# Linear attention and a feed-forward product on one core: all chunks in pairs, 64-row products side by side, earlier DMA transposes, an order that counts the queue's rows

## Chip, cores, metric

One core of a Trainium2 chip. The metric is the device time of one execution in microseconds (us), the median of several runs. The kernel before takes 196.92 us (196.65 to 197.27, 4 runs; the prediction was made against 196.75, the median of the first 3).

## The reference, cut to what matters

```python
# r, k, v, w: (4, 8, 768, 48) f32; u: (8, 48); w_in: (384, 2048); w_out: (2048, 384)
for t in range(S):                                   # per batch and head, state is 48 x 48
    cur = einsum('bhd,bhe->bhde', u * k_t, v_t)
    y[:, :, t] = einsum('bhd,bhde->bhe', r_t, state + cur)
    state = w_t[..., None] * state + einsum('bhd,bhe->bhde', k_t, v_t)
x = y.transpose(0, 2, 1, 3).reshape(3072, 384)
h = x @ w_in
out = maximum(0.01 * h, h) @ w_out
```

## The kernel before

The sequence is cut into 24 chunks of 128 steps (6 per batch entry). A chunk is done by matrix products: cumulative sums of log w, decayed r and k, their transposes, masked scores, an inner product with v, an outer product that feeds the state. The feed-forward part runs chunk by chunk beside it. Before any instruction is emitted, a small list scheduler (`Plan.order`) puts all steps of all engines in one order, from priorities and guessed durations; each engine then runs its part in that fixed order.

Chunks 0 to 5 are done as three *pairs*, 6 to 23 as *singles*. A pair loads two time steps per partition (runs of 384 B in place of 192 B), and so its time axis is interleaved: it works on two 64-row halves (`ab`) and two interleaved chunks (`j`, `jt`, `js`).

```python
NPE = 14; LEAD = 4; PAIRS = (0, 2, 4)        # DMA transposes from chunk index 14
WEIGHTS = [(2, 4.0)] * 2 + [(4, 24.0)] * 4 + [(6, 44.0)] * 2
yp_r = pp_r = ring("yp", 1, [128, 512], F32, psum)      # one bank for outer and inner
...                                          # pair(n):
for ab in range(2):                          # outer: one half, then (later) the other
    pp = yp_r.take()
    for p in range(NP):
        for j in range(2):
            nc.tensor.matmul(pp.t[:, p*2*D:(p+1)*2*D],            # 64 x 128 tile
                lhsT=rk[j].t[q0:q0+64, 1, 2*p:2*p+2, :], rhs=vb[j].t[q0:q0+64, 2*p:2*p+2, :], ...)
...
for p in range(NP):                          # scores of one jt: 32 matmuls, 64 x 64 tiles
    for js in range(2):
        for q in (0, 64):
            for par in range(2):
                nc.tensor.matmul(sc[par].t[q:q+64, p, 64*js:64*js+64], ...)
...
for ab in range(2):                          # state: 8 matmuls, 128 x 64 tiles
    for p in range(NP):
        nc.tensor.matmul(yp.t[q:q+64, 2*p*D:(2*p+2)*D], lhsT=rkT[jt].t[:, p, q:q+64], rhs=sbs[ab]..., ...)
for h in range(H):                           # inner: 32 matmuls, 64 x 64 tiles
    for js in range(2):
        for ab in range(2):
            nc.tensor.matmul(yp.t[q:q+64, h*D:(h+1)*D], lhsT=m.t[q:q+64, ...], rhs=vb[js].t[q:q+64, h, :], ...)
...                                          # single(n): 8 scores, 4 outer, 4 state, 8 inner, 128 rows each
```

## Time and profile before

| | before |
|---|---|
| time, median | 196.92 us |
| span in the profile | 195.8 us |
| TensorE busy | 180.3 us (92%) |
| first matmul, first feed-forward matmul, start of the last matmul | 4.85, 23.64, 192.03 us |
| gaps on TensorE between them | 7.2 us, all before 46.1 us |

The prediction shows the lines. How to read them: TensorE (PE) is busy nearly all the time, but its records overlap, since matmuls are pipelined (twelve L808 are shown with 0.83 us, and the next group starts 0.67 after them). What it has to issue is better read from starts: the *issue time* of a group below is the time from each matmul's start to the next one's, gaps taken off. Added up over this trace it is 180.0 us.

### The profile page before, as it was taken

The page shows a single profiled execution, that of the slowest core. Times are in us where ns is not written, and L with a number is a line of the kernel's source. Part 1 is how long each engine was busy: PE and PEld are TensorE (multiplying, and loading weights), DVE is VectorE, ACT ScalarE, POOL GpSimd, SP SyncE. Part 2 cuts the span into 40 slices and gives each one's busy share as a digit, 9 for nine tenths or more (in the row PEclk, how much of TensorE's full clock was granted, in tenths as well). Part 3 has the DMA queues.
Part 4 walks back from the last instruction along what each step waited for, and adds up shares of the span by engine and source line. Part 5 has one row for each costly group of instructions (what it writes and reads, how often), then busy time and mean ns, then how long its engine had stood idle before and what let it go on. Part 6 is the DMA issues. An engine that isn't in the chain of part 4 may idle for free.

```text
span 195.8 us, 6457 instructions
## 1 busy us (share of the span) xinstructions
PE 180.3 (92%) x2680; PEld 141.3 (72%) x2680; DVE 129.6 (66%) x228; ACT 119.2 (61%) x256; POOL 109.0 (56%) x148
## 2 busy tenths in 40 slices
PE   0978399987999999999999999999999999999993
PEld 0355398784778878877877877877878778778771
DVE  2399955599698897976768568666869676541111
ACT  3655267577665876775878675757654656334430
POOL 7598905187997999889638647547534202100000
PEclk9999759999999999999999999999999999999999
DMA  6999998999998999786487696999942614711012
GB/s 160 300 327 293 380 313 243 244 255 190 186 258 174 217 223 209 157 172 136 112 159 162 146 197 146 204 177 179 201 94 64 142 49 116 97 60 55 11 41 82
DMA packets 109280, 33.92 MB, mean 173 GB/s; under 512 B 102593, under 2 KB 107714, under 8 KB 109250
## 3 DMA queue, kind: packets, MB, share of 16 engines
q1 hardware_dynamic: 109250, 33.50, 75.8%
q8 instruction: 21, 0.34, 0.7%
q14 instruction: 9, 0.07, 0.1%
HBM read 25.17 MB, written 4.72 MB: 153 GB/s over the span
## 4 chain that ended last, share of the span: by engine, by line
PE 83%; SPq 7%; DMA 4%; DVE 3%; issue 1%; ACT 1%; DVEq 0%
PE hp L808 33%; PE op L860 32%; SPq L460 5%; DMA in<-in_moe_w_in_dram 4%; PE se L738 3%; PE yp L772 2%; PE cp L679 2%; PE so L380 1%; PE yp L642 1%; PE yp L749 1%; DVE rk L340 1%; PE yp L767 1%; PE se L380 1%; SPq L282 1%; PE yp L448 1%
## 5 line engine op out<-in xcount | busy, mean ns | idle before, releaser
L842 ACT ACTIVATE g<-hp 128x512 bf16<-128x512 f32 x96 | 57.3, 597 | 42.5 <-PE hp L808 41.7
L808 PE MATMUL hp<-xT,w_in_b 128*128 128x128 bf16 x1152 | 81.0, 221 | 0.8 <-ACT xT L455 0.8
L860 PE MATMUL op<-w_out_b,g 128*128 128x384 bf16 x384 | 77.0, 326 | 0.9 <-DVE w_out_b L305 0.9
L808 PEld LDWEIGHTS <-w_in_b 128*128 128x128 bf16 x1152 | 70.7, 99 | 8.4 <-issue 1.1
L860 PEld LDWEIGHTS <-g 128*128 128x128 bf16 x384 | 33.1, 98 | 15.0 <-issue 1.0
L361 POOL TENSOR_TENSOR vs<-in,dg 128x384 f32<-128x384 f32 x24 | 21.2, 891 | 20.9 <-DVE y L434 12.9
L349 POOL TENSOR_TENSOR ru<-in,ub 128x384 f32<-128x384 f32 x24 | 26.2, 1100 | 7.7 <-DMA in<-in_r_dram 7.7
L353 POOL TENSOR_TENSOR ru<-ru,in 128x384 f32<-128x384 f32 x24 | 26.6, 1112 | 0.4
L410 POOL TENSOR_TENSOR sb<-s,a 128x384 bf16<-128x384 f32 x15 | 13.3, 887 | 20.9 <-DVE s L424 8.9
L340 DVE TENSOR_TENSOR rk<-in,er 128x384 bf16<-128x384 f32 x24 | 18.4, 768 | 9.2 <-DMA in<-in_r_dram 5.5
L434 DVE TENSOR_TENSOR y<-yp,vs 128x384 bf16<-128x384 f32 x24 | 13.3, 555 | 12.7 <-PE yp L772 9.2
L340 DVE TENSOR_TENSOR rk<-in,ek 128x384 bf16<-128x384 f32 x24 | 21.3, 887 | 0.1
L329 POOL CAST vb<-in 128x384 bf16<-128x384 f32 x24 | 14.5, 612 | 6.2 <-issue 4.3
L876 DVE COPY o<-op 128x384 f32<-128x384 f32 x10 | 5.6, 558 | 16.9 <-PE op L860 16.7
L401 DVE TENSOR_TENSOR m<-se,maskb 128x512 bf16<-128x512 f32 x18 | 12.4, 687 | 5.6 <-PE so L738 5.4
L357 DVE TENSOR_REDUCE dg<-ru 128x8 f32<-128x384 f32 x24 | 12.8, 543 | 3.9 <-POOL ru L353 3.8
L334 ACT ACTIVATE er<-cp 128x384 f32<-128x384 f32 x21 | 10.3, 489 | 7.1 <-DVE ci L704 5.5
L324 ACT ACTIVATE lw<-in 128x384 bf16<-128x384 f32 x24 | 12.3, 520 | 2.9 <-DMA in<-in_w_dram 2.9
L704 DVE TENSOR_TENSOR ci<-cp,lw 128x384 f32<-128x384 f32 x18 | 9.9, 551 | 4.6 <-ACT xT L455 2.3
L424 DVE TENSOR_TENSOR s<-yp,sb 128x384 f32<-128x384 f32 x16 | 8.8, 552 | 5.9 <-PE yp L595 3.5
L401 DVE TENSOR_TENSOR m<-so,maskb 128x512 bf16<-128x512 f32 x18 | 12.2, 679 | 0.0
L380 PEld LDWEIGHTS <-rk 128*128 128x128 bf16 x112 | 8.6, 108 | 3.7 <-DVE rk L340 1.9
(93 smaller groups left out, 213.4 us busy)
## 6 DMA issues: line engine op xcount, KB each, us to landing
out_dram<-o SPq DMA_DIRECT2D x24, 192.0 KB, 2.2
in<-in_w_dram SPq DMA_DIRECT2D x18, 192.0 KB, 3.6
in<-in_k_dram SPq DMA_DIRECT2D x18, 192.0 KB, 3.7
in<-in_r_dram SPq DMA_DIRECT2D x18, 192.0 KB, 3.9
in<-in_v_dram SPq DMA_DIRECT2D x18, 192.0 KB, 3.7
in<-in_moe_w_in_dram SPq DMA_DIRECT2D x4, 768.0 KB, 7.6
in<-in_moe_w_out_dram SPq DMA_DIRECT2D x4, 768.0 KB, 9.6
in<-in_w_dram SPq DMA_DIRECT2D x3, 384.0 KB, 8.2
```

Of the source, the lines that this page charges most:

```text
L329: "POOL", 0.57, lambda: nc.gpsimd.tensor_copy(out=vb.t[:], in_=vn.t),
L340: lambda: nc.vector.tensor_tensor(out=rk.t[:, a, :, 0:D], in0=xn.t, in1=e.t[:], op=ALU.mult),
L349: lambda: nc.gpsimd.tensor_tensor(out=ru.t[:], in0=rn.t, in1=ubv, op=ALU.mult),
L353: lambda: nc.gpsimd.tensor_tensor(out=ru.t[:], in0=ru.t[:], in1=kn.t, op=ALU.mult),
L357: lambda: nc.vector.tensor_reduce(out=dg.t[:], in_=ru.t[:], axis=AX.X, op=ALU.add),
L361: lambda: nc.gpsimd.tensor_tensor(out=vs.t[:], in0=vn.t, in1=dg.t[:].unsqueeze(2).to_broadcast([128, H, D]), op=ALU.mult),
L401: lambda par=par: nc.vector.tensor_tensor(out=m.t[:, par], in0=sc[par].t[:], in1=mask.unsqueeze(1).to_broadcast([128, NP, 128]), op=ALU.mult),
L410: lambda: nc.gpsimd.tensor_tensor(out=sb.t[:].rearrange("p g a d -> p (g a) d"), in0=s_in.t[:].rearrange("p g a d -> p (g a) d"), in1=a_ap ...
L434: lambda: nc.vector.tensor_tensor(out=y.t[:], in0=hd(yp.t[:, 0:DM]), in1=vs.t[:], op=ALU.add),
L808: nc.tensor.matmul(hp.t[:, a * N : (a + 1) * N], lhsT=w_in_b[:, t, (j + a) * 128 : (j + a + 1) * 128], rhs=xT[:, t, c0 : c0 + N], start=(a ...
L842: lambda hp=hp, g=g, j=j, J=J, N=N: nc.scalar.activation(out=g.t[:, j : j + J, 0:N], in_=hp.t[:, 0 : J * N].rearrange("p (a n) -> p a n", ...
L860: nc.tensor.matmul(op.t[:], lhsT=g.t[:, j, off : off + 128], rhs=w_out_b[:, j, :], start=(j == 0), stop=(j == NJ - 1))
```

## The change

All chunks become pairs; the outer and state products alternate their halves, the outer's into two banks; transposes go to the DMA queue from the ninth chunk; the first pair takes banks that are still idle; weights are queued later, the row of u by ScalarE's queue; and the scheduler models a queue that holds a limited number of rows. Smaller edits of the same diff (durations in the scheduler's model, no latency between two steps of one engine, three `g` buffers in place of four) are not shown.

```diff
-            free[e] = now + self.dur[i] * (1.8 if e == "PE" and now < 18 else 1)
+            free[e] = now + self.dur[i] * (1.8 if e == "PE" and now < 26 else 1)
...
+                flying = [x for x in flying if x[0] > free[e]]
+                while sum(x[1] for x in flying) + self.rows[i] > 3300:
+                    free[e] = max(free[e], flying.pop(0)[0])
...
-    NPE = 14
-    LEAD = 4
+    NPE = 8
+    LEAD = 8
-    PAIRS = (0, 2, 4)
+    PAIRS = range(0, NCH, 2)
-    WEIGHTS = [(2, 4.0)] * 2 + [(4, 24.0)] * 4 + [(6, 44.0)] * 2
-    CASTS = 2
+    WEIGHTS = [(2, 20.15)] * 2 + [(4, 40.15)] * 4 + [(6, 44.0)] * 2
+    CASTS = 3
...
-                s_T += turn(rk[j], rkT[j], s_d[j], n, P0)
+                s_T += turn(rk[j], rkT[j], s_d[j], n, P0, (hp_r, hp_r) if j and n == 0 else (se_r, so_r))
...
+            pps = [op_r.take(), op_r.take()] if n == 0 else [se_r.take(), so_r.take()]
+            def outer():
+                for p in range(NP):
+                    for j in range(2):
+                        for ab in range(1 if last else 2):
+                            ...matmul into pps[ab], rows 64*ab to 64*ab+63...
...
-                    for ab in range(2):
-                        for p in range(NP):          # state
+                    for p in range(NP):
+                        for ab in range(2):
```

More of the change, by code (lines that the diff above doesn't have):

```diff
@@ L22, in __init__, with add @@
     def __init__(self):
-        self.eng, self.dur, self.fn, self.deps, self.pri, self.wire = [], [], [], [], [], []
-    def add(self, eng, dur, fn, deps, pri, wire=None):
+        self.eng, self.dur, self.fn, self.deps, self.pri, self.wire, self.rows = [], [], [], [], [], [], []
+    def add(self, eng, dur, fn, deps, pri, wire=None, rows=0):
         i = len(self.eng)
@@ L33, in add @@
         self.wire.append(wire)
+        self.rows.append(rows)
         return i
@@ L48, in order @@
         dma_free = 0.0
+        flying = []
         for i in range(n):
@@ L72, in order @@
             else:
+                flying = [x for x in flying if x[0] > free[e]]
+                while sum(x[1] for x in flying) + self.rows[i] > 3300:
+                    free[e] = max(free[e], flying.pop(0)[0])
                 dma_free = max(dma_free, free[e]) + self.wire[i]
                 done[i] = dma_free + 1.6
+                flying.append((done[i], self.rows[i]))
             heapq.heappush(events, (free[e], e))
@@ L77, in order @@
                 left[j] -= 1
-                ready_at[j] = max(ready_at[j], done[i])
+                same = self.eng[j] == e and self.wire[i] is None
+                ready_at[j] = max(ready_at[j], free[e] if same else done[i])
                 if not left[j]:
@@ L141 @@
     NCI = 3
-    NPE = 14
-    LEAD = 4
+    NPE = 8
+    LEAD = 8
     AHEAD = 5
-    PAIRS = (0, 2, 4)
-    PWIRE, WIRE = 1.3, 1.15
-    WEIGHTS = [(2, 4.0)] * 2 + [(4, 24.0)] * 4 + [(6, 44.0)] * 2
-    CASTS = 2
+    PAIRS = range(0, NCH, 2)
+    PWIRE, WIRE = 1.45, 1.15
+    WEIGHTS = [(2, 20.15)] * 2 + [(4, 40.15)] * 4 + [(6, 44.0)] * 2
+    CASTS = 3
     blocks = [1] * NCH
@@ L192 @@
     y_r = ring("y", 4, [128, H, D], BF16)
-    g_r = ring("g", 4, [128, NJ, max(blocks) * L], BF16)
+    g_r = ring("g", 3, [128, NJ, max(blocks) * L], BF16)
     o_r = ring("o", 4, [128, DM], F32)
     hp_r = ring("hp", 2, [128, 512], F32, psum)
-    op_r = ring("op", 2, [128, DM], F32, psum)
+    op_r = ring("op", 2, [128, 512], F32, psum)
     cp_r = ring("cp", 1, [128, 512], F32, psum)
     yp_r = pp_r = ring("yp", 1, [128, 512], F32, psum)
-    se_r = ring("se", 1, [128, NP, 128], F32, psum)
-    so_r = ring("so", 1, [128, NP, 128], F32, psum)
+    se_r = ring("se", 1, [128, 512], F32, psum)
+    so_r = ring("so", 1, [128, 512], F32, psum)
     with tc.manual_schedule():
@@ L253, with step @@
         plan = Plan()
-        def step(eng, dur, fn, pri, reads=(), writes=(), deps=(), wire=None):
+        def step(eng, dur, fn, pri, reads=(), writes=(), deps=(), wire=None, rows=0):
             d = list(deps)
@@ L259, in step @@
                 d += x.old
-            i = plan.add(eng, dur, fn, d, pri, wire)
+            i = plan.add(eng, dur, fn, d, pri, wire, rows)
             for x in (*reads, *writes):
@@ L290, in load @@
                     )
-            ld = step("SP", 0.45, load, pri, writes=[st], wire=2.0)
+            ld = step("SP", 0.45, load, pri, writes=[st], wire=2.0, rows=(384, 512)[which])
             made = []
@@ L338, in product @@
             return step(
-                "DVE", 0.6 if n < 4 else 0.84 - 0.04 * a,
+                "DVE", 0.65 if n < 2 else 0.84 - 0.04 * a,
                 lambda: nc.vector.tensor_tensor(out=rk.t[:, a, :, 0:D], in0=xn.t, in1=e.t[:], op=ALU.mult),
@@ L363, in bonus, with gt, turn @@
                 P0 + 2, reads=[vn, dg], writes=[vs], deps=[vl, s_dg])
-        def turn(rk, rkT, s_d, n, P0):
+        def gt(t):
+            return t[:].rearrange("p (g t) -> p g t", t=128)
+        def turn(rk, rkT, s_d, n, P0, banks):
             if n >= NPE:
@@ L371, in turn @@
                         out=rkT.t[:], in_=rk.t[:].rearrange("p a h d -> p (a h d)")),
-                    P0, reads=[rk], writes=[rkT], deps=s_d, wire=1.6)]
+                    P0, reads=[rk], writes=[rkT], deps=s_d, wire=1.7, rows=512)]
             made = []
             for a, eng in ((0, "DVE"), (1, "ACT")):
-                tr = (se_r, so_r)[a].take()
-                trv = tr.t[:].bitcast(BF16).rearrange("p g t -> p (g t)").rearrange("p (g t) -> p g t", t=128)
+                tr = banks[a].take()
+                trv = gt(tr.t[:].bitcast(BF16))
                 def tpose(trv=trv, a=a):
@@ L401, in masked @@
                     lambda par=par: nc.vector.tensor_tensor(
-                        out=m.t[:, par], in0=sc[par].t[:],
+                        out=m.t[:, par], in0=gt(sc[par].t),
                         in1=mask.unsqueeze(1).to_broadcast([128, NP, 128]), op=ALU.mult),
@@ L415, in shrink, with state @@
                 P0 + 1, reads=[s_in, use], writes=[sb], deps=deps)
-        def state(sx, pp, sb, P0, deps):
+        def state(sx, pp, i, sb, P0, deps):
             def f():
-                i = pp.t[:, 0:DM].rearrange("p (g a d) -> p g a d", g=NP, a=2)
                 if sb is None:
@@ L441, in finish @@
                         out=xT[:, :, col : col + L], in_=y.t[:].rearrange("p h d -> p (h d)")),
-                    P0 + 1, reads=[y], deps=[s_ye], wire=0.65))
+                    P0 + 1, reads=[y], deps=[s_ye], wire=0.65, rows=200))
                 return
@@ L460, in load_in @@
                 "SP", 0.45, lambda: nc.sync.dma_start(out=view(use), in_=src), P0 + 0.1 * i,
-                writes=[use], wire=wire, deps=[cums[n - AHEAD]] if n >= AHEAD else [])
+                writes=[use], wire=wire, rows=1024, deps=[cums[n - AHEAD]] if n >= AHEAD else [])
         def spread_u():
             u_row = step(
-                "SP", 0.45,
-                lambda: nc.sync.dma_start(out=ur[:], in_=u.rearrange("h d -> (h d)").unsqueeze(0)),
-                0.15, wire=0.05)
+                "ACT", 0.5,
+                lambda: nc.scalar.dma_start(out=ur[:], in_=u.rearrange("h d -> (h d)").unsqueeze(0)),
+                -1, wire=0.05)
             up = op_r.take()
@@ L470, in spread_u @@
                 "PE", 0.7,
-                lambda: nc.tensor.matmul(up.t[:], lhsT=onef[:], rhs=ur[:], start=True, stop=True),
-                0, writes=[up], deps=[u_row])
+                lambda: nc.tensor.matmul(up.t[:, 0:DM], lhsT=onef[:], rhs=ur[:], start=True, stop=True),
+                -1, writes=[up], deps=[u_row])
             return step(
-                "ACT", 0.5, lambda: nc.scalar.copy(out=ub[:], in_=up.t[:]), 3, reads=[up], deps=[s_ub])
+                "ACT", 0.5, lambda: nc.scalar.copy(out=ub[:], in_=up.t[:, 0:DM]), 0.05, reads=[up], deps=[s_ub])
         def weights_at(n):
@@ L571, in pair @@
             for j in range(2):
-                s_T += turn(rk[j], rkT[j], s_d[j], n, P0)
+                s_T += turn(rk[j], rkT[j], s_d[j], n, P0, (hp_r, hp_r) if j and n == 0 else (se_r, so_r))
             vs = [vs_r.take() for _ in range(2)]
             s_vs = [bonus(vs[j], rn[j], kn[j], vn[j], (kl, rl, vl), P0) for j in range(2)]
+            pps = [op_r.take(), op_r.take()] if n == 0 else [se_r.take(), so_r.take()]
[3 more added lines that the diff above has]
+                        for ab in range(1 if last else 2):
+                            q0 = 64 * ab
+                            nc.tensor.matmul(
+                                gt(pps[ab].t)[:, p, 0 : 2 * D],
+                                lhsT=rk[j].t[q0 : q0 + 64, 1, 2 * p : 2 * p + 2, :].rearrange("p h d -> p (h d)"),
+                                rhs=vb[j].t[q0 : q0 + 64, 2 * p : 2 * p + 2, :].rearrange("p a d -> p (a d)"),
+                                start=(j == 0), stop=(j == 1), skip_group_check=True)
+            s_pp = step(
+                "PE", 0.45, outer, P0 + 1, reads=[*rk, *vb], writes=pps, deps=[s_d[0][1], s_d[1][1], *s_vb])
             sbs, s_sbs = [], []
             for ab in range(2):
-                q0 = 64 * ab
                 sb, s_sb = None, []
@@ L589, in pair @@
                     break
-                pp = yp_r.take()
-                def outer(pp=pp, q0=q0):
-                    for p in range(NP):
-                        for j in range(2):
-                            nc.tensor.matmul(
-                                pp.t[:, p * 2 * D : (p + 1) * 2 * D],
-                                lhsT=rk[j].t[q0 : q0 + 64, 1, 2 * p : 2 * p + 2, :].rearrange("p h d -> p (h d)"),
-                                rhs=vb[j].t[q0 : q0 + 64, 2 * p : 2 * p + 2, :].rearrange("p a d -> p (a d)"),
-                                start=(j == 0), stop=(j == 1), skip_group_check=True)
-                s_pp = step(
-                    "PE", 0.35, outer, P0 + 1, reads=[*rk, *vb], writes=[pp],
-                    deps=[s_d[0][1], s_d[1][1], *s_vb])
+                pp = pps[ab]
                 sx = sx_r.take()
-                prev = (sx, [state(sx, pp, sb, P0, [s_pp, *s_sb])])
+                prev = (sx, [state(
+                    sx, pp, gt(pp.t)[:, :, 0 : 2 * D].rearrange("p g (a d) -> p g a d", a=2), sb, P0, [s_pp, *s_sb])])
             for jt in range(2):
-                sc = [se_r.take(), so_r.take()]
+                sc = [hp_r.take(), hp_r.take()] if jt and n == 0 else [se_r.take(), so_r.take()]
                 def scores(sc=sc, jt=jt):
@@ L617, in scores @@
                                     nc.tensor.matmul(
-                                        sc[par].t[q : q + 64, p, 64 * js : 64 * js + 64],
+                                        gt(sc[par].t)[q : q + 64, p, 64 * js : 64 * js + 64],
                                         lhsT=rkT[js].t[q0 : q0 + D, NP + p, q : q + 64],
@@ L621, in scores @@
                                         start=True, stop=True, skip_group_check=True)
-                s_sc = step("PE", 0.6, scores, P0 + 1, reads=rkT, writes=sc, deps=s_T)
+                s_sc = step("PE", 0.37, scores, P0 + 1, reads=rkT, writes=sc, deps=s_T)
                 m = m_r.take()
@@ L628, in intra @@
                 def intra(m=m, yp=yp, jt=jt):
-                    for ab in range(2):
-                        if sbs[ab] is None:
-                            continue
-                        for p in range(NP):
+                    for p in range(NP):
+                        for ab in range(2):
+                            if sbs[ab] is None:
+                                continue
                             q = 64 * ab
@@ L650, in pair @@
                 s_y = step(
-                    "PE", 0.8, intra, P0 + 1, reads=[m, *vb, rkT[jt], *there], writes=[yp],
+                    "PE", 0.62, intra, P0 + 1, reads=[m, *vb, rkT[jt], *there], writes=[yp],
                     deps=[*s_m, *s_T, *s_vb, *s_sbs[0], *s_sbs[1]])
@@ L696, in single @@
                     lambda: nc.tensor.matmul(
-                        hd(cq.t[:]), lhsT=trex[:], rhs=lw.t[:, :, 0:D], start=True, stop=True),
+                        hd(cq.t[:, 0:DM]), lhsT=trex[:], rhs=lw.t[:, :, 0:D], start=True, stop=True),
                     P0, reads=[lw], writes=[cq], deps=[s_ln])
-                ci, e_in, s_w = cq, hd(cq.t[:]), [s_cum]
+                ci, e_in, s_w = cq, hd(cq.t[:, 0:DM]), [s_cum]
             else:
@@ L713, in single @@
             rkT = rkT_r.take()
-            s_T = turn(rk, rkT, [s_r, s_k], n, P0)
+            s_T = turn(rk, rkT, [s_r, s_k], n, P0, (se_r, so_r))
             vs = vs_r.take()
@@ L738, in scores @@
                         nc.tensor.matmul(
-                            sc[par].t[:, p, :], lhsT=rkT.t[q0 : q0 + D, NP + p, :],
+                            gt(sc[par].t)[:, p, :], lhsT=rkT.t[q0 : q0 + D, NP + p, :],
                             rhs=rkT.t[q0 : q0 + D, p, :], start=True, stop=True, skip_group_check=True)
@@ L760, in single @@
                 sx = sx_r.take()
-                prev = (sx, [state(sx, pp, sb, P0, [s_pp, *s_sb])])
+                prev = (sx, [state(
+                    sx, pp, pp.t[:, 0:DM].rearrange("p (g a d) -> p g a d", g=NP, a=2), sb, P0, [s_pp, *s_sb])])
             yp = yp_r.take()
@@ L860, in down @@
                         nc.tensor.matmul(
-                            op.t[:], lhsT=g.t[:, j, off : off + 128], rhs=w_out_b[:, j, :],
+                            op.t[:, 0:DM], lhsT=g.t[:, j, off : off + 128], rhs=w_out_b[:, j, :],
                             start=(j == 0), stop=(j == NJ - 1))
@@ L871 @@
                         s_o = step(
-                            "ACT", 0.5, lambda o=o, op=op: nc.scalar.copy(out=o.t[:], in_=op.t[:]),
+                            "ACT", 0.5, lambda o=o, op=op: nc.scalar.copy(out=o.t[:], in_=op.t[:, 0:DM]),
                             3, reads=[op], writes=[o], deps=[s_dn])
@@ L875 @@
                         s_o = step(
-                            "DVE", 0.56, lambda o=o, op=op: nc.vector.tensor_copy(out=o.t[:], in_=op.t[:]),
+                            "DVE", 0.56, lambda o=o, op=op: nc.vector.tensor_copy(out=o.t[:], in_=op.t[:, 0:DM]),
                             3, reads=[op], writes=[o], deps=[s_dn])
@@ L881 @@
                             out=rows[ch], in_=o.t[:]),
-                        5, reads=[o], deps=[s_o], wire=0.55)
+                        5, reads=[o], deps=[s_o], wire=0.55, rows=128)
         for n in range(NCH):
```

## The prediction

> **What bounds the kernel now.** I read the page first (engine shares, the 40 slices, the costly groups), then TensorE's waits, then the timeline of each engine from 0 to 50 us, and last the timeline of TensorE in the steady part. On the page TensorE is the busiest engine, and its two costliest groups are the two products of the feed-forward part, L808 and L860.
>
> ```profile
> PE 180.3 (92%) x2680; PEld 141.3 (72%) x2680; DVE 129.6 (66%) x228; ACT 119.2 (61%) x256; POOL 109.0 (56%) x148
> ...
> PE   0978399987999999999999999999999999999993
> ...
> PEclk9999759999999999999999999999999999999999
> ```
>
> The second line shows where TensorE is not full: slices 1 to 10 (4.9 us each, so the first 49 us) and the last. The third shows a granted clock of 0.7 and 0.5 in slices 5 and 6. TensorE's waits say the same: after 50 us there is none.
>
> ```profile
> PE cp L511 <- POOL pmask L232: 4.8, 1, 4.8
> PE yp L448 <- DVE y L434: 3.2, 1, 3.2
> PE op L860 <- DVE w_out_b L305: 0.9, 1, 0.9
> PE hp L808 <- ACT xT L455: 0.8, 2, 0.6
> PE se L617 <- DVE rkT L388: 0.8, 1, 0.8
> ```
>
> The hole of 3.2 us is in front of the first feed-forward product, and what follows it is cold:
>
> ```profile
> 22.20 0.50 PE L448 MATMUL yp<-ident,y 128*128 128x128 bf16 x3 [3.18 <-DVE y L434]
> 22.79 0.58 PE L380 MATMUL se<-ident,rk 128*128 128x128 bf16 x4
> 23.64 1.44 PE L808 MATMUL hp<-xT,w_in_b 128*128 128x128 bf16 x12 [0.27 <-ACT xT L455]
> ```
>
> Twelve of these products take 1.44 us here; in the steady part they are issued in 0.67. The full rate is back at about 28.4 us. VectorE's timeline shows why y is late: it sits, in VectorE's fixed order, behind four products of the next pair that run at 1.2 to 1.4 us each.
>
> ```profile
> 17.46 0.56 DVE L340 TENSOR_TENSOR rk<-in,er 128x384 bf16<-128x384 f32 x1 [0.32 <-DMA in<-in_r_dram]
> 17.94 1.36 DVE L340 TENSOR_TENSOR rk<-in,ek 128x384 bf16<-128x384 f32 x1
> 19.23 1.35 DVE L340 TENSOR_TENSOR rk<-in,er 128x384 bf16<-128x384 f32 x1
> 20.50 1.18 DVE L340 TENSOR_TENSOR rk<-in,ek 128x384 bf16<-128x384 f32 x1
> 21.60 0.54 DVE L434 TENSOR_TENSOR y<-yp,vs 128x384 bf16<-128x384 f32 x1
> ```
>
> So: from 50 us to the last matmul at 192.0 us TensorE issues without a gap, and the end is set by how much it has to issue plus what it loses before 50 us. From the starts of successive matmuls between 50 and 170 us: L808 56.6 ns, L860 166 ns, so the feed-forward part is 1152 x 56.6 + 384 x 166 = 129 us. The attention adds, by the same spacings and the counts of the groups, about 41.5 us at full rate (a chunk alone: cumulative sums 0.27, scores 8 x 41 ns = 0.33, outer product 4 x 42 = 0.17, state 0.17, inner 8 x 27 = 0.22, and with TensorE's transposes 8 x 56 = 0.45 and 3 x 57 = 0.17 more). 192.4 - 170.5 leaves 21.9 us lost: 4.9 before the first matmul, 7.1 in later gaps, the rest slow matmuls before 28.4 us.
>
> **What the Trainium skill says.** "TensorE: Matmul & The Clock Gate", Part 1, says that the array runs at half rate until about 3.4 us of sustained work, and falls back after an idle window of that length; the trace agrees (3.18 us of gap, then 1.44 against 0.67 us). "TensorEngine Tiling (Array Packing)", Tiling Modes and Gotcha 1, says that two 64-row tiles can run in parallel but must not write one PSUM bank at once. The trace agrees as far as it can: the scores, which rotate over four tiles and two banks, are spaced at 12 ns, while the 64-row outer products L595, one half after the other into one bank, are spaced at 55 ns. "DMA: Bandwidth & Descriptors", DMA Transpose, allows the transpose for 2-byte data from this queue; in this trace ten of each kind already run, rkT landing after a median of 3.4 us and xT after 2.3.
>
> **The change, part by part.** (1) *All chunks in pairs.* Chunks 6 to 23 go from 18 singles to 9 pairs. A pair in this trace costs TensorE: sums 2 x 168 + 8 x 25 ns = 0.54; outer 16 x 55 = 0.88; scores 64 x 12 = 0.76; state 16 x 38 = 0.60; inner 64 x 17 = 1.1. That is 3.9 us against 2 x 1.16 for two singles, since a pair works in 64x64 tiles, twice as many for scores and four times as many for the inner product.
> (2) *Side by side.* The outer product alternates its two row halves into two banks, and the state product its two column halves. I estimate two at a time at the present spacing of one: outer 8 x 55 = 0.44, state 0.35 to 0.45. A new pair is then 3.1 to 3.25 us; nine of them, less the halved outer product in the three last pairs of a sequence, 26.5 to 28.5 us, where the 18 singles (without the parts that first and last chunks lack) are 19.4. So plus 7 to 9 us. The three old pairs give back 1.5 to 2.
> (3) *DMA transposes from the ninth chunk instead of the fifteenth.* Six chunks lose 0.45 + 0.17 us: minus 3.7. VectorE and ScalarE lose six copies of 0.4 and 0.6 us, off the path. The queue has 12 more transposes at 1.2 to 2.3 us of issue, in a part where it has time, as loads come in half as many issues.
> (4) *TensorE's sum* of 1 to 3: plus 1 to 4 us, I take 2.4. The change costs on the bounding engine.
> (5) *The start.* The order now counts the queue's rows in flight, weights come after the second pair's first two loads, the row of u comes by ScalarE's queue, and pair 0 uses the idle hp and op banks. In the listed order VectorE now does y of chunk 0 before the next pair's products and before any weight cast. I work it forward on the present durations: the four products of pair 0 end near 10 us (10.5 now), the casts of 1.1 us each leave the chain, the four masks with their two states take until about 16.5, y ends near 17.6 instead of 22.1, so the first L808 starts near 19 to 20 instead of 23.6. ScalarE no longer holds xT behind a cast that waits 4.2 us for a weight load. Gain about 4 us, of which some goes back, as the matmuls between 19 and about 26 us would run at half rate (the changed order's own table assumes so until 26): I count 3.
> (6) *20 to 50 us.* Loads land one after another at 1.5 us for a pair's and 2.1 us for a weight block. In the new order of issue the third pair is complete near 33 us (now 41), the fourth near 44 (now its second half near 47), and the weights near 38 (now 43). The 2.0 us of gaps between 29 and 50 us should mostly go, and slow spots with them: 2 to 2.5.
>
> Sum: +2.4 - 3 - 2.3 = -2.9 us, so 196.75 - 2.9, about 193.8; I put 193.6.
>
> **The rivals.** *A: the start gains more.* If TensorE stays at full rate from 18.4 us on, where its matmuls were fast just before the hole, another 2 to 3 us go, and side by side may pair better than I took (the plan's own 0.62 us for an inner step is less than my 0.72 to 0.75). Then 189 to 191. For it: the hole itself caused the cold stretch. Against: the table's 26 us. *B: the pair's arithmetic eats it.* With no overlap in the outer and state products, part 1 is worth plus 12 us and the time would be 197 to 199. Against: separate banks and different tiles, and the scores already do it. *C: a new wait.* Every pair now takes the single se and so banks up to five times (two transposes, outer, two scores), and the outer's bank is held through state 0.55, shrink 0.9, state 0.55 us. Summed with VectorE's masks of 0.69 that is 7 to 9.5 us for a pair, against a pair's period of about 13 us, so it should hide; in the start, where attention runs eight chunks ahead, it may not, and a gap over 3 us would cost the clock as well: 195 to 198. *D: the transposes by DMA come late* behind loads in the one queue; eight chunks of lead instead of four hide it.
>
> **Range and chances.** The two big terms have opposite signs and each is uncertain by 2 us: TensorE's added work is sure in sign, the start's gain sure in sign too. That gives 189.0 to 197.2. The line for faster by 2% is 192.8, just under my middle; since the change looks tuned as a whole, the long side is the fast one: faster 0.43, same 0.51, slower 0.06.
>
> **What would show it.** The first feed-forward product should start at 19 to 20.5 us, with no gap over 1.5 us on TensorE before it after 5 us, and TensorE without gaps from about 25 us. The outer group should show 16 per pair at about 28 ns spacing, and TensorE's issue time from 50 us on should per chunk be longer than now in the DMA-transposed part (1.55 us of attention against 1.16). Wrong it would be if gaps on TensorE return after 50 us with VectorE's masks, states or rkT transposes as releasers, if the first L808-like product starts after 22 us, or if the outer product keeps 55 ns.

## The result, and the profile after

Ratios here are the mean time of one kernel's fast runs over that of the kernel before in the same rounds, so they are not quite the ratio of the medians quoted. Three medians quoted below contain one slow run each; over the fast runs they are 191.98 (three pairs), 204.90 (the state's halves) and 212.79 us (no count of rows).

| | before | after |
|---|---|---|
| time, median | 196.92 us | 204.64 us (204.37 to 205.73, 4 runs) |
| ratio | | 1.040 (95%: 1.036 to 1.044), slower |
| first matmul | 4.85 us | 2.40 us |
| first feed-forward matmul | 23.64 us | 20.12 us |
| TensorE's issue time | 180.0 us | 188.0 us |
| gaps after the first matmul | 7.2 us | 8.35 us |
| start of the last matmul | 192.03 us | 198.79 us |

The page of the changed kernel, engine shares and slices:

```profile
span 202.5 us, 8257 instructions
...
PE 188.4 (93%) x3610; PEld 145.9 (72%) x3610; DVE 127.9 (63%) x222; ACT 111.4 (55%) x232; POOL 108.6 (54%) x148
...
PE   3788859899999999999999979999999999999993
...
PEclk9999999999999999999999999999999999999999
```

TensorE's slices look better than before: full from the ninth on but for one 7 (a wait of 1.1 us for a DMA transpose, below). The row of the granted clock looks better too, but it misleads: its first record in this trace begins at 23.45 us, the slices before it are printed as full, and the matmuls tell otherwise. Twelve L821 take 1.46 us at 20.12 and 0.83 at 23.45 (below), and the first outer group takes 0.75 us against 0.45 later. TensorE was thus slow until 23.45 us. In the kernel before it was slow until 18.6 and again from 22.0 to 28.9. The matmuls issued while it was slow took 17.2 us of issue, against 18.4 before: hardly less. What grew is TensorE's count of matmuls, from 2680 to 3610; no other engine has more to do. TensorE's waits in the changed kernel:

```profile
PE op L481 <- DMA ur<-in_u_dram: 2.4, 1, 2.4
PE hp L821 <- DVE w_in_b L313: 2.0, 2, 1.1
PE se L629 <- DMA rkT<-rk: 1.1, 1, 1.1
PE op L873 <- DVE w_out_b L313: 1.1, 2, 0.7
PE cp L521 <- ACT lw L332: 1.0, 1, 1.0
```

The hole of 3.2 us is gone; in its place stand waits for the casts of weights and, once, for a DMA transpose. The start of the feed-forward part, from TensorE's timeline:

```profile
20.12 1.46 PE L821 MATMUL hp<-xT,w_in_b 128*128 128x128 bf16 x12
...
23.45 0.83 PE L821 MATMUL hp<-xT,w_in_b 128*128 128x128 bf16 x12
...
25.84 0.84 PE L821 MATMUL hp<-xT,w_in_b 128*128 128x128 bf16 x12 [1.11 <-DVE w_in_b L313]
...
28.33 1.51 PE L821 MATMUL hp<-xT,w_in_b 128*128 128x128 bf16 x24 [0.92 <-DVE w_in_b L313]
```

The start went as the prediction drew it: first product at 20.12 us, full rate at 23.5. And yet the end is 6.8 us later. The difference of the two ends splits exactly into TensorE's own terms: attention without transposes 36.3 to 47.6 us (+11.4), transposes -4.0, feed-forward +0.65, first matmul -2.45, gaps +1.1. The first matmul is now the row of u, though; attention's first one is at 5.05 us, 0.2 later than before, and 1.0 of the gaps lies between the two.

Where the 11.4 us come from shows when an inner step of each kind is set side by side in the steady part, from TensorE's timelines. Before, a single chunk's state and inner product (L767, L772):

```profile
93.46 0.83 PE L808 MATMUL hp<-xT,w_in_b 128*128 128x128 bf16 x12
94.13 0.33 PE L767 MATMUL yp<-sb,rkT 128*128 128x96 bf16 x4
94.30 0.36 PE L772 MATMUL yp<-vb,m 128*128 128x48 bf16 x8
94.51 0.81 PE L860 MATMUL op<-w_out_b,g 128*128 128x384 bf16 x4
```

After, the same for one chunk of a pair (L646, L654):

```profile
136.05 0.81 PE L873 MATMUL op<-w_out_b,g 128*128 128x384 bf16 x4
136.80 0.36 PE L646 MATMUL yp<-sb,rkT 128*64 128x96 bf16 x4
137.09 0.69 PE L654 MATMUL yp<-vb,m 64*64 64x48 bf16 x32
137.70 0.84 PE L821 MATMUL hp<-xT,w_in_b 128*128 128x128 bf16 x12
```

Read the starts. The single needs 94.51 - 94.13 = 0.38 us. The paired chunk needs 137.70 - 136.80 = 0.90 us, and the group ahead of it is longer too: four L873 are 0.65 us when another 128-row group follows, here 0.75. Means over the steady part, per group, start to the next group's start:

| | two singles | one pair |
|---|---|---|
| sums | 0.54 | 0.54 |
| outer | 8 matmuls, 0.34 | 16, 0.45 (8, 0.44 where only one half is needed) |
| scores | 16, 0.66 | 2 x (32, 0.38) |
| state | 8, 0.34 | 2 x (8, 0.29; 4, 0.29 where only one half is needed) |
| inner | 16, 0.43 | 2 x (32, 0.62) |
| sum | 2.30 us | 3.56 us |

Two rows are odd: half the matmuls of the outer or the state product take just as long as all of them. So the halves do overlap, but each group also has a fixed cost. From the last state matmul's start to the next group's start it is 0.135 us, in a stream of one shape (a single's state product, 128x128 tiles) 0.042. A pair has seven groups with such an end, two singles have two (their scores).

### The profile page after: what moved, and what is told of

Read it like the earlier page. It is cut to its first block, busy times and chain, and to the rows that moved or that the text cites. A ratio compares the mean times of both kernels' runs of the same rounds, so it can differ in the third digit from the quotient of the medians.

```text
span 202.5 us, 8257 instructions
## 1 busy us (share of the span) xinstructions
PE 188.4 (93%) x3610; PEld 145.9 (72%) x3610; DVE 127.9 (63%) x222; ACT 111.4 (55%) x232; POOL 108.6 (54%) x148
## 4 chain that ended last, share of the span: by engine, by line
PE 76%; DMA 11%; SPq 9%; DVE 1%; issue 0%
PE op L873 29%; PE hp L821 29%; SPq L470 7%; PE yp L654 6%; DMA in<-in_moe_w_out_dram 4%; DMA in<-in_moe_w_in_dram 4%; DMA rkT<-rk 3%; PE yp L646 3%; SPq L290 2%; PE se L629 2%; PE se L594 2%; PE cp L521 2%; PE so L629 1%; PE cp L531 1%; PE so L391 1%; PE yp L458 0%
## 5 line engine op out<-in xcount | busy, mean ns | idle before, releaser
L821 PE MATMUL hp<-xT,w_in_b 128*128 128x128 bf16 x1152 | 80.3, 220 | 2.0 <-DVE w_in_b L313 2.0
L821 PEld LDWEIGHTS <-w_in_b 128*128 128x128 bf16 x1152 | 70.5, 98 | 11.5 <-DVE w_in_b L313 2.3
L873 PE MATMUL op<-w_out_b,g 128*128 128x384 bf16 x384 | 77.4, 326 | 1.1 <-DVE w_out_b L313 1.1
L873 PEld LDWEIGHTS <-g 128*128 128x128 bf16 x384 | 33.1, 98 | 15.2 <-issue 1.3
L421 POOL TENSOR_TENSOR sb<-s,pa 128x384 bf16<-128x384 f32 x20 | 18.8, 938 | 22.7 <-DVE s L434 9.1
L369 POOL TENSOR_TENSOR vs<-in,dg 128x384 f32<-128x384 f32 x24 | 20.1, 847 | 15.9 <-DVE dg L365 15.9
L348 DVE TENSOR_TENSOR rk<-in,er 128x384 bf16<-128x384 f32 x24 | 21.5, 897 | 5.6 <-DMA in<-in_r_dram 5.4
L412 DVE TENSOR_TENSOR m<-se,pmask 128x512 bf16<-128x512 f32 x23 | 15.8, 685 | 9.8 <-PE so L629 9.7
L654 PE MATMUL yp<-vb,m 64*64 64x48 bf16 x768 | 17.3, 191 | 0.0
L654 PEld LDWEIGHTS <-m 64*64 64x64 bf16 x768 | 14.7, 113 | 1.7
L412 DVE TENSOR_TENSOR m<-so,pmask 128x512 bf16<-128x512 f32 x23 | 15.6, 680 | 0.0
L629 PEld LDWEIGHTS <-rkT 48*64 48x64 bf16 x768 | 9.0, 111 | 3.7 <-issue 1.9
L629 PE MATMUL se<-rkT,rkT 48*64 48x64 bf16 x184 | 10.0, 196 | 1.1 <-DMA rkT<-rk 1.1
```

The source lines that it names most:

```text
L348: lambda: nc.vector.tensor_tensor(out=rk.t[:, a, :, 0:D], in0=xn.t, in1=e.t[:], op=ALU.mult),
L369: lambda: nc.gpsimd.tensor_tensor(out=vs.t[:], in0=vn.t, in1=dg.t[:].unsqueeze(2).to_broadcast([128, H, D]), op=ALU.mult),
L412: lambda par=par: nc.vector.tensor_tensor(out=m.t[:, par], in0=gt(sc[par].t), in1=mask.unsqueeze(1).to_broadcast([128, NP, 128]), op=ALU.m ...
L421: lambda: nc.gpsimd.tensor_tensor(out=sb.t[:].rearrange("p g a d -> p (g a) d"), in0=s_in.t[:].rearrange("p g a d -> p (g a) d"), in1=a_ap ...
L629: nc.tensor.matmul(gt(sc[par].t)[q : q + 64, p, 64 * js : 64 * js + 64], lhsT=rkT[js].t[q0 : q0 + D, NP + p, q : q + 64], rhs=rkT[jt].t[q0 ...
L654: nc.tensor.matmul(yp.t[q : q + 64, h * D : (h + 1) * D], lhsT=m.t[q : q + 64, h % 2, h // 2, 64 * js : 64 * js + 64], rhs=vb[js].t[q : q ...
```

## The experiments

Fourteen kernels; each is compared with the kernel before on the same chip. The theory (theory 1): TensorE's issue in pairs costs the time. The rivals: the DMA transposes and the one queue (theory 2), the new order or the lead of eight chunks (theory 3).

**Undoing one part each.** Three pairs only, on the changed kernel:

```diff
-    PAIRS = range(0, NCH, 2)
+    PAIRS = (0, 2, 4)
```

> The changed kernel with only the first three pairs left, chunks 6 to 23 single again; transposes by DMA from the ninth chunk, new order and idle banks stay. Theory 1 (TensorE has more to issue in pairs): nine pairs at 3.64 us of issue less three half outer products are about 32 us, the singles they replace 19.4, so 12.6 us fall away: 192 us (190 to 194). Theory 2 (the DMA transposes and the one queue hold TensorE up): they stay and the loads get shorter runs, so 202 or more. Theory 3 (the new order or the lead of eight chunks costs): 202 or more.

Measured: 192.21 us, ratio 0.976 (0.970 to 0.981). In the trace the last matmul starts at 186.16 us, 12.6 us before the changed kernel's, the amount counted beforehand. Theories 2 and 3 fall as causes of the loss, since all that they name is still in this kernel. With the old transposes on top (`NPE = 14`):

> As the kernel with three pairs, but DMA transposes only from the fifteenth chunk, so only order, idle banks and side by side differ from the kernel before. Theory 1: six chunks of TensorE transposes come back at 0.62 us each, 196 us (194 to 197.5). Theory 2: faster than the kernel with three pairs and early DMA transposes. Theory 3: 200 or more.

Measured: 194.49 us, ratio 0.987 (0.982 to 0.992). What is left of the change here (start, order, banks, side by side in three pairs) gives about 2.5 us. The changed kernel with only `NPE = 14`:

> The changed kernel with DMA transposes only from the fifteenth chunk; pairs everywhere stay. Theory 1: TensorE gets 3.7 us more, 208 us (206 to 210). Theory 2 (late DMA transposes are what costs): 201 or less.

Measured: 207.11 us, ratio 1.053 (1.047 to 1.058): the early DMA transposes help by 2.5 us, not quite the 3.7 expected. And the kernel before with only `PAIRS = range(0, NCH, 2)`:

> The kernel before with all chunks in pairs and nothing else. Theory 1: nine old pairs at 3.9 us, less a half outer product in three, are 34 us against 19.4: plus 14 to 15 us, 211 us (208 to 214). Theories 2 and 3: half the load packets, no new transposes and the old order, so 195 to 198.

Measured: 214.43 us, ratio 1.090 (1.085 to 1.095), 17.6 us more than before by the ratio, where 14 to 15 were expected. Attention's issue rose by 14.6 us, as expected; 1.9 more came in the feed-forward part. Its outer products take 9.6 us of issue, the changed kernel's 5.9: side by side is worth 3.7 us, less than a third of what the pairs cost.

**Which halves overlap, and what a group costs.** The changed kernel with the state's halves one after the other:

```diff
-                    for p in range(NP):
-                        for ab in range(2):
+                    for ab in range(2):
+                        for p in range(NP):
```

> The changed kernel with the state product's two column halves one after the other again (four matmuls, then four), all else kept. If the prediction's step were right (side by side works two at a time), this would cost 0.2 us in each of 21 of the 24 inner steps, plus 4 us: 208 to 209. If column halves do not overlap (the trace after has 42 to 45 ns each side by side, the one before 38 ns one after the other), it is the same or up to 1 us faster: 203.5 to 205.

Measured: 205.31 us, ratio 1.046 (1.041 to 1.051), against 1.040 (1.036 to 1.044): the same. A state group of 8 takes 0.301 us this way and 0.291 the other. The second range came true, but not for its reason: as four matmuls of one half alone take 0.287 us, the halves overlap in either order, and did so in the kernel before. There was nothing to win. The same edit for the outer product:

> The changed kernel with the outer product's two row halves one after the other, still in two banks. If row halves overlap (28 to 33 ns side by side against 55 ns in the kernel before), the eight full pairs lose 16 x 25 ns each, plus 3 us: 207 to 208.5. If the gain came from the banks alone, the same: 204.6.

Measured: 205.30 us, ratio 1.049 (1.045 to 1.053). That lies between the two values expected, and the interval begins just above the end of the changed kernel's (1.044), on another chip: the loss, under 2 us, is barely shown by the time alone. Its trace is clear on the group, though: 16 outer matmuls take 0.63 us here against 0.45 side by side and twice 0.44 in the kernel before. Part of the gain thus comes from having one group in two banks and part from alternating. TensorE's issue rose by 1.2 us, and its gaps were 1.9 us smaller than in the changed kernel's trace, which hid it.

The decisive one for the fixed cost splits each inner step in two rounds, the same matmuls in another order:

```diff
+                    for part in range(2):
-                    for p in range(NP):                 # state
+                        for p in range(2 * part, 2 * part + 2):
-                    for h in range(H):                  # inner
+                        for h in range(4 * part, 4 * part + 4):
```

> The changed kernel with the inner step's matmuls in another order: state of two head pairs, inner of four heads, state of the other two, inner of the other four. The same matmuls, two more changes of tile shape in each of 24 inner steps (each side has the state's 128x64 and the inner's 64x64 tiles). If a group's end costs a fixed 0.10 to 0.13 us that the next shape has to wait for (the traces have 0.135 us from the last state matmul's start to the next group's, against 0.042 in a stream of one shape), plus 48 x 0.1, some 4 to 6 us: 208.5 to 211. If each matmul costs its mean spacing, whatever stands beside it, the same: 204 to 205.5.

Measured: 208.55 us, ratio 1.060 (1.055 to 1.065), about 3.9 us above the changed kernel; TensorE's issue rose by 5.4 us, which over 48 more changes of shape is 0.11 us each (gaps that were 2.1 us smaller hid some of it in the time). Its timeline:

```profile
99.41 0.81 PE L874 MATMUL op<-w_out_b,g 128*128 128x384 bf16 x4
100.15 0.27 PE L647 MATMUL yp<-sb,rkT 128*64 128x96 bf16 x2
100.36 0.43 PE L655 MATMUL yp<-vb,m 64*64 64x48 bf16 x16
100.72 0.27 PE L647 MATMUL yp<-sb,rkT 128*64 128x96 bf16 x2
100.92 0.37 PE L655 MATMUL yp<-vb,m 64*64 64x48 bf16 x12
```

A round of half as many state matmuls takes 0.21 us, not half of 0.29; half of the inner ones take 0.36, not half of 0.62. The Trainium skill, "TensorEngine Tiling (Array Packing)", Key Properties, says that changing the tiling mode "drains the TensorE"; these traces agree and give the size. So of the 1.26 us that a pair costs more than two singles, 0.5 to 0.55 us are five more of these groups at 0.1 to 0.11 us, an estimate from this run. The rest, about 0.7 us, is put down to more matmuls by subtraction, and nearly all of it is the inner product: without its two ends it takes about 1.0 us with 64 matmuls, against 0.43 with 16. No run takes that part away.

**Fewer pairs, earlier weights, earlier transposes, shorter lead**, all on the version with three pairs. `PAIRS = (0, 2)`:

> The changed kernel with only the first two pairs left. If a pair's extra TensorE issue of 1.3 us is all that counts, chunks 4 and 5 as singles make it 1 to 1.5 us faster than three pairs: 190.5 to 191.5. If the loads of the start bind (runs of 192 B in place of 384 B), it is the same or slower: 192 to 194.

Measured: 194.01 us, ratio 0.990 (0.984 to 0.996). Issue fell by 1.2 us as counted, but TensorE's gaps grew from 9.1 to 11.3 us. Only 0.9 of that lies before 50 us; 1.3 are waits of singles for VectorE after 142 us. So the third pair pays, but not only in the start, and why is not shown. The weights' old priorities:

> Three pairs, but the weight loads queued as early as in the kernel before (and the casts still at the later priority). If the weights' late arrival (2.6 us of TensorE waits for the casts of w_in) is what eats the gain of the start, it is 1.5 to 2.5 us faster: 189.5 to 190.5. If the second pair's loads, now later, cost as much as that, it is the same or slower: 192 to 194.

Measured: 192.87 us, ratio 0.985 (0.980 to 0.989): no gain. The waits for w_in went from 2.6 us to none among the longest, and a wait of 2.7 us for w_out and one of 1.7 us for the state came. Near the end of the first of these, at 37.6 us, the granted clock fell to 0.5 until 44.4 us, which may have eaten a gain. `NPE = 6`:

> Three pairs, DMA transposes already from the seventh chunk. Theory 1 (TensorE's issue sets the end): two chunks less at 0.62 us each, 191 us (190.3 to 191.7). If the queue, full in the start, delivers those transposes late, the same or slower than three pairs from the ninth chunk: 192 to 194.

Measured: 192.81 us, ratio 0.981 (0.977 to 0.986): no gain that could be told apart from the version with three pairs. Issue fell by 0.9 us; gaps grew by 0.6, none of them behind a DMA transpose. `LEAD = 4`:

> Three pairs, with a lead of four chunks as in the kernel before. If the lead matters (DMA transposes late, attention late), it is slower: 193.5 or more. If TensorE's sum is all that counts, the same: 191.5 to 193.

Measured: 193.11 us, ratio 0.979 (0.975 to 0.984): just outside the range for no effect, and not to be told apart from the version with three pairs.

**What holds the start back.** Three pairs, with most of the weight loads taken away (casts of blocks 1 to 3 read block 0; wrong, relative error 1.76):

```diff
+                if q:
+                    v = w_in_v[:, 0, q*512 : q*512+48] if which == 0 else w_out_v[:, q*JQ, 0:48]
+                    nc.sync.dma_start(out=st.t[:, 0:48], in_=v)
```

> Three pairs, result wrong on purpose: only the first of the four blocks of each weight is loaded, the other six loads shrink to 24 KB and the casts read the first block, in the same order of instructions. If the queue's landings bound the stretch from 20 to 45 us (weights complete near 39.9 us, TensorE waiting 2.6 us for the casts of w_in), the waits for casts go and the time falls by 2.5 to 5 us: 187 to 189.7. If the attention's chain through VectorE and GpSimd bounds that stretch, less than 1 us: 191 to 192.5.

Measured: 190.09 us, ratio 0.966 (0.963 to 0.969), 2 us below three pairs, between the two ranges set beforehand (2.5 to 5, and less than 1). But the gain is not in the waits: 8.8 us of gaps on TensorE stay (9.1 with all loads), 1.3 of them still for a cast of w_in, the others small waits for products, sums and y. Of the 1.8 us by which the last matmul starts earlier in the trace, 1.5 are issue, and TensorE was slow there until 15.0 and from 18.4 to 21.8 us, with all loads until 18.1 and from 28.4 to 31.8. Whether the landings gave the 2 us, or the moment at which the rate rose, is not shown. Next, the first pair on the ordinary banks:

```diff
-(hp_r, hp_r) if j and n == 0 else (se_r, so_r)
+(se_r, so_r)
-pps = [op_r.take(), op_r.take()] if n == 0 else [se_r.take(), so_r.take()]
+pps = [se_r.take(), so_r.take()]
-sc = [hp_r.take(), hp_r.take()] if jt and n == 0 else [se_r.take(), so_r.take()]
+sc = [se_r.take(), so_r.take()]
```

> Three pairs, but the first pair uses the se and so banks for all of its transposes, outer product and scores, as the later pairs do. If the idle banks are what moves the first feed-forward product from 23.6 to 20 us, that product starts 1.5 to 3 us later and the time rises to 194 to 195.5. If the first pair waits for VectorE's and GpSimd's work rather than for banks, or the loads of the weights set the pace anyway, under 1 us: 191.5 to 193.

Measured: 191.43 us, ratio 0.970 (0.969 to 0.972), the lowest median of a correct kernel, though its interval overlaps that of three pairs (0.970 to 0.981). TensorE's timeline of its start:

```profile
26.17 1.22 PE L821 MATMUL hp<-xT,w_in_b 128*128 128x128 bf16 x12
27.22 0.33 PE L458 MATMUL yp<-ident,y 128*128 128x128 bf16 x3
```

The first feed-forward product starts 6.6 us later than with idle banks (19.6 us), and the end is no later: 185.7 against 186.2 us for the last matmul. TensorE was slow until 27.0 us here, so attention's work filled the slow stretch, and nearly all of the feed-forward part ran at full rate. Last, again with three pairs and the idle banks, the order without the count of rows, `> 3300` made `> 10**9`:

> Three pairs, the order worked out without the limit on rows in flight. If counting the queue's depth gives the order its value, waits for casts and products in the start grow and the time rises to 194 or more. If the order of the start hardly depends on it (it lists the same first 60 groups on TensorE), 191.5 to 193.

Measured: 213.12 us, ratio 1.085 (1.077 to 1.092). I had expected the smaller value from looking at the first part of the order only. The loss is not in the start. TensorE's waits:

```profile
PE se L750 <- DMA rkT<-rk: 7.4, 1, 7.4
PE yp L785 <- DVE m L412: 5.9, 6, 1.6
```

and the slices of its page:

```profile
PE   3697789999999999344059999999999999999993
...
PEclk9997979999999999755559999999999999999999
```

Between 84 and 110 us TensorE runs nearly dry and then cold. The queue's timeline in that stretch has eight loads in a row, an output, four more loads and another output, all between one transpose and the next, for which the scores wait:

```profile
88.91 1.30 SPq L381 DMA_TRANSPOSE rkT<-rk  x1
...
103.58 1.28 SPq L381 DMA_TRANSPOSE rkT<-rk  x1
```

The end of that stretch:

```profile
98.35 1.28 POOL ru L357
99.62 0.60 SPq L470
100.28 1.63 SPq L470
102.00 0.66 SPq L470
102.75 0.72 SPq L893
103.58 3.64 DMA rkT<-rk
107.26 0.28 PE se L750
```

These are pieces of its chain that ended last: a product on GpSimd, four issues on the queue, the transpose, and then the scores. With loads free to issue, the scheduler put too many of them ahead of the transpose. What the count of rows gives here is in the middle of the kernel, not in its start. The kernel before has no such count either, and no gap after 46.1 us: the count matters together with the rest of the change (early transposes, lead of eight, the new model), and no run separates these.

## Why the prediction was wrong

It said 193.6 us, 189.0 to 197.2; it was 204.64. By its own parts:

1. *Pairs (parts 1 and 2): the step that failed first.* The sign was right, the size was not. It had 3.1 to 3.25 us for a new pair and 26.5 to 28.5 us for nine; measured are 3.56 us, and 32.0 us for nine (19.4 plus the 12.6 by which the version with three pairs ends earlier). The terms: the state product was put at 0.35 to 0.45 us "two at a time at the present spacing of one", and is 0.58. The spacing of 38 ns that it halved was a mean over 8 matmuls whose halves already overlapped, with a fixed end of group in it. The halved outer products of the last pairs save nothing (0.44 against 0.45). The inner product is 1.24, not 1.1: with the ends of its groups, its matmuls take 19 ns each, not 17. Only the outer product came out as put (0.45 against 0.44): its 55 ns had the end in it too, but its halves were two groups (each 0.308 us and an end of 0.135) and became one (0.311 and 0.135), so that the halving held for both. The prediction's own terms add up to 3.19 to 3.29 us and 28 to 29 us for nine, so 0.5 to 1.5 us were lost in the sum as well.
2. *The old pairs* gave back about 1.25 us of issue in place of 1.5 to 2.
3. *Transposes (part 3):* -4.0 us of issue against -3.7, right, though in time it is 2.5 us.
4. *Feed-forward:* nothing was put down; it is +0.65 us, at least in part because the group ahead of a change of shape waits for it (0.75 against 0.66 us above).
5. *TensorE's sum (part 4)* was thus +8.1 us and not +2.4: 5.7 of the miss of 11.0.
6. *Start and 20 to 50 us (parts 5 and 6): the second step that failed.* -5.3 us was expected; first matmul and gaps together gave -1.3 in the changed kernel, another 4.0 of the miss (the rest is rounding, and two profiled runs that lie 6.8 us apart where the medians lie 7.7). Every event that was drawn came true within 2 us: the first product at 20.12 us, the third pair's loads complete at 34.6, the fourth's at 45.2, the weights at 39.5. Wrong was the value put on them. An earlier first feed-forward product is worth nothing by itself, as the run without idle banks shows: TensorE may do other work first, and only its gaps and slow stretches count. Of those, the one hole went and many small ones came, so that the gaps before 50 us add up to 7.3 us, as before (7.2); and the slow stretch issued 17.2 us of matmuls in place of 18.4. In the reading of the hole, three of the four products that held y back took 1.2 to 1.4 us, the first 0.56. And the trace agrees on the clock less closely than the prediction says: the gap, 3.18 us, is shorter than the 3.4 us it names, and with most weight loads taken away the granted clock fell at 18.4 us with no gap over 0.9 us in the ten before it.
7. *The rivals.* B was nearest: "the pair's arithmetic eats it", put at 197 to 199. Its reason, no overlap, was not the cause: overlap was there, for the state product already before the change. Its sum is wrong too: by the prediction's own terms part 1 is plus 14.4 us, not 12, which with the other parts unchanged gives about 202. C's new wait showed once, 1.1 us. D's late transposes cost no more than that here, but the last experiment shows, on three pairs, how near they are: the lead of eight alone does not hide them.

Left open: why the gaps before 50 us stay near 8 us when the weights' loads are nearly gone. They are small waits for VectorE's and ScalarE's steps, and no run here took those away one by one. Open too is what sets the moment at which TensorE's rate rises: for good at 21.8 us in one trace and at 31.8 in another.

## What to carry to other kernels

Before splitting a product into smaller tiles, count groups and not only matmuls: each change of tile shape cost 0.11 us here, so a mean spacing must not be halved before first-to-last and last-to-next have been read apart. On an engine that is full to the end, ask of each part only what it adds to that engine's issue or takes from its gaps; when some first event comes earlier, that alone is no gain. And an order fixed beforehand should count what an in-order queue can hold, above all when transposes that TensorE waits for share it with bulk loads: leaving the count out cost 21 us here.

## What the Trainium skill lacked or had wrong

- "TensorEngine Tiling (Array Packing)", Key Properties, says that a change of tiling mode drains TensorE but gives no size: here 0.11 us for each of 48 added changes, and 0.135 us from the last start of a 128x64 group to the next group's start, against 0.042 us in a stream of one shape.
- "TensorE: Matmul & The Clock Gate", Back-to-back issue gap, gives about 81 ns per matmul for a sustained stream of weight load and matmul at 128 columns; here 837 such pairs of the kernel before, from 50 to 170 us, run at 56.6 ns on average, close to its figure for the isolated gap.
- Same page, Part 1, says that start to start never drops below about 25 ns, and does not say there that this holds for one tile only: the 64x64 scores, spread over four tiles, start 3 to 43 ns apart, 12 on average with the group's end. (Its Part 3 has the short steps between tiles.)
- "DMA: Bandwidth & Descriptors" has no figure for how long a queue with many rows in flight holds its issuer on this chip: the first load's issue took 0.45 us, a later one 5.46 us (22.74 to 28.20 us in the changed kernel), and on three pairs an order worked out without the count of rows lost 21 us.
